# Transposes of the second pair's second norm moved from TensorE to DMA, and a scheduler's price for two-operand work on VectorE set to zero from one point on

## The chip, the cores and the metric

The kernel runs on one core of a Trainium2 chip. A core has TensorE (PE in the profile, its weight loads PEld), VectorE (DVE), ScalarE (ACT), GpSimd (POOL) and SyncE (SP), which here issues all DMAs. The metric is device time of one execution in microseconds (us); of several runs the median counts.

## The reference, cut to what matters

One transformer block with conditioned layer norms, attention over a window of 512 cached keys, and a gated feed forward. Softmax, gelu and silu are the usual ones; c is one row of 512 values.

```python
mod = (silu(c) @ w_mod) -> sa, ca, ga, sb, cb, gb        # six rows of 512
h = layernorm(x) * (1 + ca) + sa                          # x: 2048 x 512
q = h @ wq                                                # 32 heads of 128
s = q @ k[last 512].T / sqrt(128);  p = softmax(s);  o = p @ v[last 512]
x = x + ga * (o @ wo)
h = layernorm(x) * (1 + cb) + sb                          # the second norm
x = x + gb * ((gelu(h @ w_gate) * (h @ w_up)) @ w_down)   # 1376 hidden columns
```

## The kernel before, in words

Every large product runs on TensorE in fp16, with each fp32 operand split into a high part and a low part (value minus high part) and three products for one: high by high, high by low, low by high. Making the parts is work for the other engines. The usual split is a copy to fp16 on ACT and a subtraction of two tensors that lie in SBUF; the function `tt` leaves it to the scheduler whether POOL or DVE does that subtraction.

The 2048 rows are four quarters (`qg` 0 to 3) of 512; quarters 0, 1 are pair 0 and 2, 3 are pair 1. Attention goes over 128 iterations of (head, quarter). An iteration has four times 12 matmuls of 128x512: scores into `psS`, values into `psO`, the output projection into `psW`, the next q into `psQ`. DVE takes the maximum of the scores (`st<-psS`), ACT the exponentials, POOL the low parts of the probabilities (`pp`, 128x1024), SP turns them by DMA transposes (`pT`), DVE and ACT split `oT`, and DVE adds each `psW` to the sum in SBUF (`acc<-psW,st,acc`). There are two banks of `psW`, two pairs of `psS`, one bank of `psO` and of `psQ`: a late evacuation stops TensorE. Beside this the weights of coming heads are scaled, split, and for heads from 2 on combined for a Strassen-Winograd form (`a_sum`, `a_split`, `t_full`, `t_sum`, tiles S, A, tf, T, B).

A weight's scale comes from its largest value over all partitions: the maxima go to DRAM and come back to every partition (`sa`), DVE reduces them (`top`), makes a bounded factor `iv` of four values (line 673) and its reciprocal `av` (line 674). This happens 29 times.

The feed forward works on a pair of quarters at a time. For the second norm of quarters 2 and 3 `ln2_norm` writes the normalized rows in fp32 into tiles of the set T; `ln2_chunk` has TensorE transpose four 128x128 pieces into `psQ`, and ACT or DVE applies the column factors to the result (`hf<-psQ,cols`), then comes the split. It is called through `chunk2` from the table `P1`, in the units of the first pair (lines 1843 to 1847).

Nothing is issued as it is called. The class `Weaver` records every instruction with the tiles it touches, plays the whole program forward by estimated durations, some dozens of times with small random shifts of the urgencies, keeps the play in which most matmul work is done by a number of marks, and issues in that order. Two rules matter here. An instruction may have two engines (`either`); `sooner` holds it back from one engine when the other would end it earlier. And two-operand work on DVE whose operands both lie in SBUF, and all work on POOL, is marked as using one shared port (`lock`): the play lets neither start while the other holds it, and where POOL's instruction follows DVE's closely, it is made to wait for it. To such work on DVE `sooner` adds SHY, 1500 ns, so that DVE gets it only if POOL would end it that much later.

All rows of the profile name line 444, where the recorded instructions are issued, so groups are told apart by their tiles.

Of the kernel before, what the change touches and what calls it, by code (L numbers as in the profile page):

```python
# [10 lines left out]
F32 = mybir.dt.float32  # L11
# [7 lines left out]
P = 128  # L19
N = 512  # L20
# [69 lines left out]
class Weaver:  # L90
# [159 lines left out]
    def play(self, at, users, span, keep, cut):  # L250
# [22 lines left out]
        def sooner(n, e, t):  # L273

            kinds = self.ops[n][4]
            mine = max(t, shared[e] if kinds[e][1] else 0.0) + kinds[e][0] + (e == "DVE" and kinds[e][1]) * self.SHY
            for o, kind in kinds.items():
                s = max(free[o], ready[n], shared[o] if kind[1] else 0.0)
                if o != e and s + kind[0] + (o == "DVE" and kind[1]) * self.SHY < mine:
                    return max(s, t) + 1.0  # L280
            return None

# [169 lines left out]
def adaln_block(ctx: ExitStack, tc: tile.TileContext, x, k_cache, v_cache, wq, wo,  # L452
# [82 lines left out]

    MV, RS, NMR, LNP, LNF = {}, {}, {}, {}, {}

    def ln_stats(key, src, j):
        if j == 0:
            MV[key] = base.tile([P, 4, 2], F32, name="mv", tag="mv", bufs=4)  # L540
            RS[key] = small(base, 4, 4, "rs")
        st = small(base, 6, 2, "bnst")
        nc.vector.bn_stats(st, src)
        nc.vector.bn_aggr(MV[key][:, j, :], st)
        if j == 3:
            ve = small(base, NC, 2, "ve")
            nc.gpsimd.tensor_tensor(ve, MV[key][:, :, 1], eps_t[:, :NC], op=OP.add)
            nc.gpsimd.tensor_tensor(RS[key], ve, eps_t[:, NC:], op=OP.pow)
            nm = NMR[key] = small(base, 4, 4, "nmr")
            nc.gpsimd.tensor_tensor(nm, MV[key][:, :, 0], RS[key], op=OP.mult)  # L550
            nc.gpsimd.tensor_scalar(nm, nm, -1.0, 1.0, op0=OP.mult, op1=OP.mult)
# [115 lines left out]
    def spread_max(t, top):  # L667
        w = right.tile([P, N], F32, name="sa", tag="sa", bufs=1)
        nc.sync.dma_start(w, t.rearrange("p a -> (p a)").partition_broadcast(P))
        r = small(base, 4, 2, "top")  # L670
        nc.vector.tensor_reduce(r, w.rearrange("p (k a) -> p a k", a=4), op=OP.max, axis=AX.X)
        iv, av = small(base, 8, 5, "iv"), small(base, 8, 5, "av")
        nc.vector.tensor_scalar(iv[:, 0:4], r, 1e-30, ROUND / top, op0=OP.max, op1=OP.mult)
        nc.vector.reciprocal(av[:, 0:4], iv[:, 0:4])
        return iv, av

# [592 lines left out]
    def ff_scalars(part):  # L1269
# [12 lines left out]
        if part == 2:  # L1282
            nc.vector.tensor_scalar_mul(t, t, HID)
            nc.vector.reciprocal(ffs[:, 4:5], t)
            nc.vector.reciprocal(ffs[:, 8:9], ab)
            nc.vector.tensor_scalar(cols[:, 8:16], cols[:, 8:16], ffs[:, 8:9], HS, op0=OP.mult, op1=OP.mult)

    s = max(s, 2 * (NIT - 16))
# [49 lines left out]

    N2, FULL, FB, FRAW, AW, WD, WGU, PGU, HID_T, RT, UV, PX = ({} for _ in range(12))
    PLAIN = 2  # L1340
    SLOTS = ("q", "q", "q", "k16", "A1", "A1", "raw2", "raw2")
    SBUFS = {"q": 3, "k16": 1, "A1": 2, "raw2": 2}
    WDTAG = ("kT", "v", "wo", "kT", "kT", "v", "v", "wo", "wo", "oT", "oT")
# [14 lines left out]
        return t[:, 0, c % 2, :], t[:, 1, c % 2, :]  # L1358

    def ln2_stats(qg, j):  # L1360
        ln_stats(("2", qg), acc[4 * qg + j], j)

    def ln2_norm(qg, j):
        if j % 2 == 0:
# [450 lines left out]
        f_low(p, c, "T4")  # L1815

    def chunk2(qg, c):
        ln2_chunk(qg, c)
        ln2_high(qg, c)
        ln2_low(qg, c, nc.vector)  # L1820

# [16 lines left out]
    for c in range(2):  # L1838
# [2 lines left out]


    P1 = {2: [(ln2_stats, 2, j) for j in range(4)] +
          [(ln2_norm, 2, j) for j in range(4)] + [(chunk2, 2, c) for c in range(4)],
          3: [(ln2_stats, 3, j) for j in range(4)] +
          [(ln2_norm, 3, j) for j in range(4)] + [(chunk2, 3, c) for c in range(4)],
          4: [(sums_a, 1, c) for c in range(2)] + [(sums_b, 1, c) for c in range(2)]}
    WDS = list(range(PLAIN, NF))
    left = {(p, h): 2 if h < NF // 2 else 1 for p in range(2) for h in range(NF // 2 + 1)}
# [75 lines left out]
```

## Time and profile before

| | |
|---|---|
| median of 3 runs | 1657.41 us (1656.83 to 1659.0) |
| the profiled execution | 1657.58 us, its span 1655.8 us |
| granted TensorE clock, mean | 0.997 |
| PE busy | 1642.4 us, 99% |
| DVE, ACT, POOL busy | 1289.3, 1216.6, 1305.0 us (78, 73, 79%) |

The span runs from the first to the last instruction. TensorE is busy from start to end, and the other engines are each at about three quarters: what counts is how many instructions TensorE has, and whether one of the others makes it wait. The attention goes from about 40 to 1312 us, the feed forward from there on; in it DMA has little to do.

### The profile page before, as it was taken

What the parts mean: (1) busy time and instruction counts of PE and PEld (TensorE: products, weight loads), DVE (VectorE), ACT (ScalarE), POOL (GpSimd) and SP (SyncE); (2) the same over time, 40 slices, a digit from 0 to 9 for tenths busy, and PEclk for the clock granted to TensorE, in tenths of its full rate; (3) what the DMA queues carried; (4) which work ended last, traced back from release to release, by engine and by line L of the source; (5) the groups of instructions that cost most, each with busy time, mean ns of one, the idle gap of its engine ahead of it and who ended that gap; (6) DMA issues with size and microseconds to landing.
All of it is one profiled execution on the core that took longest, in us unless ns stands there. A gap on an engine that the chain in (4) does not pass through costs nothing.

```text
span 1655.8 us, 24293 instructions
## 1 busy us (share of the span) xinstructions
PE 1642.4 (99%) x7732; PEld 764.5 (46%) x7732; DVE 1289.3 (78%) x2381; ACT 1216.6 (73%) x2418; POOL 1305.0 (79%) x1097
## 2 busy tenths in 40 slices
PE   8999999999999999999999999999999999999999
PEld 4444444444444444444444444444444444444455
DVE  7777787878787788788999887888887956656557
ACT  5987797777787777888778777787878876545451
POOL 5999986868586878787768889999977898784682
PEclk9999999999999999999999999999999999999999
DMA  7676697878787778999999997788877712101111
GB/s 241 128 144 130 135 157 143 152 138 149 144 143 140 153 136 157 186 196 194 196 200 205 189 167 148 147 175 179 168 129 158 144 28 64 42 25 51 42 45 52
DMA packets 686289, 228.61 MB, mean 138 GB/s; under 512 B 596432, under 2 KB 663056, under 8 KB 686160
## 3 DMA queue, kind: packets, MB, share of 16 engines
q1 hardware_dynamic: 686160, 227.05, 69.1%
q8 instruction: 61, 1.00, 0.3%
q14 instruction: 68, 0.56, 0.1%
HBM read 78.98 MB, written 5.38 MB: 51 GB/s over the span
## 4 chain that ended last, share of the span: by engine, by line
PE 91%; ACT 2%; POOL 2%; DVE 2%; DMA 1%; SPq 1%; issue 1%; DVEq 0%; POOLq 0%; ACTq 0%
PE psS L444 31%; PE psW L444 23%; PE psO L444 21%; PE psQ L444 17%; SPq L444 1%; DVE st L444 1%; DVE acc L444 1%; DMA pT<-pp 1%; ACT p L444 0%; POOL pp L444 0%; POOL B L444 0%; DMA wm<-in_w_mod_dram 0%; POOL aw L444 0%; ACT T L444 0%; DMA raw<-in_B_w_up_dram 0%
## 5 line engine op out<-in xcount | busy, mean ns | idle before, releaser
L444 POOL TENSOR_TENSOR pp<-p,pp 128x1024 f16<-128x1024 f32 x256 | 545.9, 2132 | 212.8 <-ACT pp L444 97.3
L444 ACT ACTIVATE p<-psS,st,es 128x512 f32<-128x512 f32 x512 | 393.4, 774 | 187.7 <-DVE st L444 186.8
L444 DVE SCALAR_TENSOR_TENSOR acc<-psW,st,acc 128x512 f32<-128x512 f32 x496 | 367.2, 742 | 79.8 <-PE psW L444 77.7
L444 PE MATMUL psW<-wo,oT 128*128 128x512 f16 x1536 | 416.3, 379 | 0.0
L444 PE MATMUL psS<-kT,q 128*128 128x512 f16 x1536 | 379.1, 379 | 2.0 <-ACT q L444 2.0
L444 PE MATMUL psO<-pT,v 128*128 128x512 f16 x1536 | 377.1, 379 | 0.3 <-DMA pT<-pp 0.2
L444 DVE TENSOR_REDUCE st<-psS 128x2 f32<-128x1024 f32 x256 | 312.5, 1221 | 60.0 <-PE psS L444 59.6
L444 ACT ACTIVATE pp<-p 128x1024 f16<-128x1024 f32 x256 | 271.0, 1059 | 3.7
L444 PEld LDWEIGHTS <-q 128*128 128x128 f16 x1536 | 149.9, 98 | 182.1 <-ACT q L444 2.6
L444 PEld LDWEIGHTS <-v 128*128 128x128 f16 x1536 | 150.0, 98 | 181.3 <-DMA pT<-pp 1.2
L444 PEld LDWEIGHTS <-oT 128*128 128x128 f16 x1536 | 150.2, 98 | 180.1 <-DVE oT L444 0.5
L444 PEld LDWEIGHTS <-aw 128*128 128x128 f16 (+1 forms) x840 | 84.2, 100 | 95.1 <-issue 2.0
L444 ACT ACTIVATE oT<-psO 128x512 f16<-128x512 f32 x128 | 76.1, 594 | 66.2 <-PE psO L444 66.1
L444 PE MATMUL psQ<-T,S 128*128 128x512 f16 x504 | 123.3, 379 | 0.0
L444 PE MATMUL psQ<-B,A 128*128 128x512 f16 x480 | 119.6, 381 | 0.1
L444 PE MATMUL psS<-T,aw 128*128 128x512 f16 (+1 forms) x480 | 116.9, 379 | 0.0
L444 DVE SCALAR_TENSOR_TENSOR oT<-psO,oT 128x512 f16<-128x512 f32 x128 | 88.0, 688 | 30.9 <-ACT oT L444 30.6
L444 PEld LDWEIGHTS <-A 128*128 128x128 f16 x696 | 68.3, 98 | 83.3 <-issue 2.3
L444 PEld LDWEIGHTS <-S 128*128 128x128 f16 x672 | 65.8, 98 | 79.3
L444 ACT ACTIVATION_READ_ACCUMULATOR p<-psS,st,es 128x1 f32 x512 | 101.0, 197 | 0.0
L444 POOL TENSOR_TENSOR q<-h,q 128x512 f16<-128x512 f32 x84 | 97.5, 1161 | 2.0 <-ACT q L444 1.8
L444 DVE TENSOR_REDUCE mx<-raw 128x1 f32<-128x512 f32 x128 | 84.2, 674 | 15.6 <-DMA raw<-in_A_wq_dram 9.1
(211 smaller groups left out, 2295.6 us busy)
## 6 DMA issues: line engine op xcount, KB each, us to landing
raw<-in_A_k_cache_dram SPq DMA_DIRECT2D x32, 256.0 KB, 3.9
raw<-in_A_wq_dram SPq DMA_DIRECT2D x32, 256.0 KB, 3.7
raw<-in_A_v_cache_dram SPq DMA_DIRECT2D x32, 256.0 KB, 3.3
raw<-in_A_wo_dram SPq DMA_DIRECT2D x32, 256.0 KB, 3.2
pT<-pp SPq DMA_TRANSPOSE x512, 3.3
sa<-most SPq DMA_DIRECT2D x29, 256.0 KB, 3.8
raw<-in_B_w_gate_dram SPq DMA_DIRECT2D x24, 256.0 KB, 3.1
raw<-in_B_w_up_dram SPq DMA_DIRECT2D x24, 256.0 KB, 3.4
```

Source lines behind the costliest of these rows:

```text
L444: made[n] = real(*a, **k)
```

## The change

There are three parts.

First, `chunk2` and the table `P1` use new functions for quarters 2 and 3. `turned_norm` normalizes into a tile of the ring p32 (already scaled by HS), copies the high part on ACT and subtracts the low part (POOL or DVE); `turned` has SP transpose both parts by DMA, 16 transposes in all, straight into the tiles that will later hold the feed forward's operand; `turned_chunk` applies the column factors to low and high part (one instruction on ACT or DVE, then a SCALAR_TENSOR_TENSOR on DVE), after which the split is made again as before.

Second, SHY counts only for instructions recorded before `nc.calm`, and `nc.calm` is set to the number of instructions recorded so far. Third, `iv` is made on POOL, while `top` and `av` stay on DVE.

```diff
-            mine = max(t, shared[e] if kinds[e][1] else 0.0) + kinds[e][0] + (e == "DVE" and kinds[e][1]) * self.SHY
+            mine = max(t, shared[e] if kinds[e][1] else 0.0) + kinds[e][0] + (e == "DVE" and kinds[e][1]) * (self.SHY if n < self.calm else 0.0)
...
-                if o != e and s + kind[0] + (o == "DVE" and kind[1]) * self.SHY < mine:
+                if o != e and s + kind[0] + (o == "DVE" and kind[1]) * (self.SHY if n < self.calm else 0.0) < mine:
...
+            if big:
+                nc.gpsimd.tensor_scalar(RS[key], RS[key], HS, 1.0, op0=OP.mult, op1=OP.mult)
...
-        nc.vector.tensor_scalar(iv[:, 0:4], r, 1e-30, ROUND / top, op0=OP.max, op1=OP.mult)
+        nc.gpsimd.tensor_scalar(iv[:, 0:4], r, 1e-30, ROUND / top, op0=OP.max, op1=OP.mult)
         nc.vector.reciprocal(av[:, 0:4], iv[:, 0:4])
...
     PLAIN = 2
+    nc.calm = len(nc.ops)
...
+    def turned_norm(qg, j):
+        if j % 2 == 0:
+            t = b_tile(0, N2TAG[qg][j // 2], (P, 2, 2, 2, N // 2))
+            N2[qg, j], N2[qg, j + 1] = t[:, 0], t[:, 1]
+            RT["norm"] = right.tile([P, 2, N], F32, name="hf", tag="p32", bufs=2)
+        n, t = RT["norm"][:, j % 2, :], N2[qg, j]
+        nc.either((S_, V), lambda o: ln_norm(("2", qg), n, acc[4 * qg + j], j, o))
+        n = n.rearrange("p (a n) -> p a n", a=2)
+        nc.scalar.activation(t[:, :, 0, :], n, AF.Copy)
+        tt(t[:, :, 1, :], n, t[:, :, 0, :], OP.subtract)
+
+    def turned(qg, j):
+        for half in range(2):
+            nm = (("B11", "B21"), ("T4", "B22"))[qg % 2][half]
+            d = ff_b(qg // 2, nm).rearrange("p a c n -> p (a c) n")
+            nc.sync.dma_start_transpose(d[:, :, j * P:(j + 1) * P], N2[qg, j][:, half].rearrange("p a n -> p (a n)"))
+
+    def turned_chunk(qg, c):
...
+        hi, lo = f_view(qg, c)
+        affine(full, lo, a, b)
+        nc.vector.scalar_tensor_tensor(full, hi, a, full, op0=OP.mult, op1=OP.add)
...
     def chunk2(qg, c):
-        ln2_chunk(qg, c)
+        turned_chunk(qg, c)
...
-          [(ln2_norm, 2, j) for j in range(4)] + [(chunk2, 2, c) for c in range(4)],
+          [(g, 2, j) for j in range(4) for g in (turned_norm, turned)] + [(chunk2, 2, c) for c in range(4)],
```

The line `nc.calm = ...` stands where the functions of the feed forward begin. The attention's iterations are recorded further down, by the loop over `slot(i)`; so what is recorded before `nc.calm` is the loads and the work ahead of the first iteration, and the attention lies behind it.

The scheduler makes of this a new order for the whole program. Three places are shown; in names a tile's buffer numbers are mostly left out. On PE, at the end of the attention, the old program has the first of the 32 transposes of quarters 2 and 3 (T_0_3045 and T_0_3046 are quarter 2's normalized rows):

```order
12207 L444 MATMUL psW<-wo,oT 128x512
12208 L444 MATMUL psQ<-ident,T_0_3045 128x128 x2
12209 L444 MATMUL psQ<-ident,T_0_3046 128x128
12210 L444 LDWEIGHTS oT
12211 L444 MATMUL psW<-wo,oT 128x512
```

In the new program no matmul of PE reads these; on SP's queue stand the first 8 of the 16 DMA transposes (T_0_3045 and T_0_3049 are the split rows of quarter 2, B_0_3047 and B_0_3048 the operand), between loads of later weights:

```order
503 L444 DMA_TRANSPOSE B_0_3047<-T_0_3045 128x4x128
504 L444 DMA_TRANSPOSE B_0_3048<-T_0_3045 128x4x128
505 L444 DMA raw<-in_B_w_gate_dram 128x4x128
506 L444 DMA raw<-in_B_w_up_dram 128x4x128
507 L444 DMA raw<-in_B_w_down_dram 128x512
508 L444 DMA raw<-in_B_w_gate_dram 128x4x128
509 L444 DMA raw<-in_B_w_up_dram 128x4x128
510 L444 DMA_TRANSPOSE B_0_3047<-T_0_3045 128x4x128
511 L444 DMA_TRANSPOSE B_0_3048<-T_0_3045 128x4x128
```

The work has changed its engine, and a load behind a transpose on SP now also waits for the split that the transpose reads. The second place is DVE between the 17th and the 18th maximum of the scores, early in the attention; before:

```order
159 L444 TENSOR_REDUCE st<-psS 128x2
160 L444 SCALAR_TENSOR_TENSOR q<-psQ,q 128x512
161 L444 TENSOR_SCALAR st<-st,es 128x1 x2
162 L444 TENSOR_SCALAR acc<-psW,st 128x512
163 L444 SCALAR_TENSOR_TENSOR acc<-psW,st,acc 128x512
164 L444 TENSOR_REDUCE st<-psS 128x2
```

And between the same two maxima now:

```order
185 L444 TENSOR_REDUCE st<-psS 128x2
186 L444 TENSOR_TENSOR tf<-tf 128x512
187 L444 TENSOR_SCALAR st<-st,es 128x1 x2
188 L444 SCALAR_TENSOR_TENSOR acc<-psW,st,acc 128x512
189 L444 TENSOR_TENSOR T_0_90<-tf,T_0_90 128x512
190 L444 TENSOR_TENSOR T_0_88<-tf,T_0_88 128x512
191 L444 SCALAR_TENSOR_TENSOR acc<-psW,st,acc 128x512
192 L444 TENSOR_TENSOR tf<-B_1_93 128x512
193 L444 TENSOR_REDUCE st<-psS 128x2
```

Four sums and splits of the Winograd tiles, which were POOL's, stand on DVE between the evacuations. Counted over the order, DVE has 4 such two-operand instructions (both operands in SBUF, 256 columns or more) in the attention before and 208 now (158 of 512 columns, 50 of 256), 49 of them ahead of the 33rd maximum; in the feed forward it has 87 before and 175 now. POOL goes from 1102 instructions to 862. The third place is POOL around the third of the 29 factors `iv`, between two `pp` of the softmax:

```order
122 L444 TENSOR_TENSOR q<-h_508,q 128x512
123 L444 TENSOR_TENSOR pp<-p_553,pp 128x2x512
124 L444 TENSOR_SCALAR iv<-top 128x4
125 L444 TENSOR_TENSOR pp<-p_567,pp 128x2x512
126 L444 TENSOR_SCALAR raw<-raw,av 128x512 x3
```

And DVE around its reciprocal:

```order
336 L444 TENSOR_REDUCE top<-sa 128x4
337 L444 TENSOR_REDUCE st<-psS 128x2
338 L444 RECIPROCAL av<-iv 128x4
339 L444 TENSOR_SCALAR st<-st,es 128x1 x2
340 L444 SCALAR_TENSOR_TENSOR oT<-psO,oT 128x512
```

`top`, `iv` and `av` followed each other on DVE; now DVE's `av` waits for POOL. Between `top` and `av` stand 0 to 14 other instructions, in 9 of the 29 cases one or none.

## Rows read from the trace of the kernel before

**Rows 1.** The page's busy times: us, share of the span, instructions.
```profile
PE 1642.4 (99%) x7732; PEld 764.5 (46%) x7732; DVE 1289.3 (78%) x2381; ACT 1216.6 (73%) x2418; POOL 1305.0 (79%) x1097
```
**Rows 2.** Stretches: length, busy PE, PEld, DVE, ACT, POOL, clock, DMA share, GB/s.
```profile
0.00:40.00 40.00, 33.54 (x156) 20.08 (x156) 29.06 (x76) 20.76 (x35) 20.25 (x40) 0.91 0.80 250
40.00:200.00 160.00, 158.88 (x752) 73.91 (x753) 120.15 (x234) 134.61 (x267) 155.21 (x119) 1.00 0.70 131
40.00:1312.00 1272.00, 1270.61 (x5900) 577.36 (x5901) 1043.29 (x1993) 1007.24 (x2033) 1041.88 (x785) 1.00 0.83 159
...
1360.00:1600.00 240.00, 239.03 (x1129) 111.64 (x1127) 142.34 (x194) 133.31 (x256) 179.03 (x205) 1.00 0.16 46
```
**Rows 3.** Waits of PE: for what, us in total, times, longest.
```profile
PE psS L444 <- POOL B L444: 0.6, 1, 0.6
PE psS L444 <- ACT r L444: 0.5, 1, 0.5
...
PE psS L444 <- DVE r L444: 0.4, 1, 0.4
```
**Rows 4.** Groups of PE: the transposes of quarters 0, 2 and 3.
```profile
L444 PE MATMUL psQ<-ident,T 128*128 128x128 f32 x48 | 8.1, 275 | 0.0
```
**Rows 5.** Timeline of PE around the last transposes: start, us.
```profile
1416.36 0.60 PE L444 MATMUL psQ<-ident,T 128*128 128x128 f32 x4
1416.80 0.59 PE L444 MATMUL psW<-wd,hid 128*128 128x512 f16 x2
```
**Rows 6.** DVE by tile r and hid: ns shortest/median/longest.
```profile
L444 DVE TENSOR_TENSOR r<-psS,h x60: 676/691/693, 1358.0 to 1635.0; 128x512 f32<-128x512 f32 x54, 96x512 f32<-96x512 f32 x6
L444 DVE TENSOR_TENSOR hid<-r,hid x36: 675/692/1534, 1340.6 to 1643.3; 128x512 f16<-128x512 f32 x32, 96x512 f16<-96x512 f32 x4
L444 DVE SCALAR_TENSOR_TENSOR r<-r,ffs x32: 737/751/1746, 1374.5 to 1641.5; 128x512 f32<-128x512 f32 x28, 96x512 f32<-96x512 f32 x4
```
**Rows 7.** Timeline of DVE and POOL in the feed forward.
```profile
1453.27 1.15 POOL L444 TENSOR_TENSOR T<-hf,T 128x512 f16<-128x512 f32 x1
1453.95 1.02 DVE L444 SCALAR_TENSOR_TENSOR r<-r,ffs 128x512 f32<-128x512 f32 x1
...
1455.11 1.27 POOL L444 TENSOR_TENSOR ft<-ft,hf 128x512 f32<-128x512 f32 x1 [0.69 <-DVE r L444]
...
1455.67 1.27 DVE L444 TENSOR_TENSOR hid<-r,hid 128x512 f16<-128x512 f32 x1
```
**Rows 8.** Timeline of DVE, POOL and PE ahead of PE's wait of 0.60 us.
```profile
1340.63 1.42 DVE L444 TENSOR_TENSOR hid<-r,hid 128x512 f16<-128x512 f32 x1
...
1341.46 1.61 POOL L444 TENSOR_TENSOR T<-hf,T 128x512 f16<-128x512 f32 x1
...
1344.14 1.16 POOL L444 TENSOR_TENSOR B<-hf,B 128x512 f16<-128x512 f32 x1
...
1345.35 0.59 PE L444 MATMUL psS<-B,B 128*128 128x512 f16 x2 [0.60 <-POOL B L444]
```
**Rows 9.** Groups of POOL: busy us, mean ns, idle before.
```profile
L444 POOL TENSOR_TENSOR pp<-p,pp 128x1024 f16<-128x1024 f32 x256 | 545.9, 2132 | 212.8 <-ACT pp L444 97.3 <-issue 91.9 <-DVE acc L444 4.5
L444 POOL TENSOR_TENSOR q<-h,q 128x512 f16<-128x512 f32 x84 | 97.5, 1161 | 2.0 <-ACT q L444 1.8 <-DVE st L444 0.2
```
**Rows 10.** Groups of DVE: addition from psW, score maximum, two-operand work, and iv.
```profile
L444 DVE SCALAR_TENSOR_TENSOR acc<-psW,st,acc 128x512 f32<-128x512 f32 x496 | 367.2, 742 | 79.8 <-PE psW L444 77.7
L444 DVE TENSOR_REDUCE st<-psS 128x2 f32<-128x1024 f32 x256 | 312.5, 1221 | 60.0 <-PE psS L444 59.6
...
L444 DVE TENSOR_TENSOR hid<-r,hid 128x512 f16<-128x512 f32 x32 | 28.3, 897 | 4.3 <-ACT hid L444 4.1
...
L444 DVE TENSOR_SCALAR iv<-top 128x4 f32<-128x4 f32 x29 | 6.1, 211 | 0.0
```
**Rows 11.** DMA issues: count, median us to landing.
```profile
pT<-pp SPq DMA_TRANSPOSE x512, 3.3
```
**Rows 12.** Groups of ACT: a split's high part.
```profile
L444 ACT ACTIVATE T<-hf 128x512 f16<-128x512 f32 x16 | 10.0, 624 | 3.1 <-POOL hf L444 2.9
```

More of the change, by code (lines that the diff above doesn't have):

```diff
@@ L536, in adaln_block, with ln_stats @@
     MV, RS, NMR, LNP, LNF = {}, {}, {}, {}, {}
-    def ln_stats(key, src, j):
+    def ln_stats(key, src, j, big=False):
         if j == 0:
@@ L1285, in ff_scalars @@
             nc.vector.reciprocal(ffs[:, 8:9], ab)
+            nc.vector.tensor_scalar_mul(ffs[:, 9:13], cols[:, 8:12], ffs[:, 8:9])
             nc.vector.tensor_scalar(cols[:, 8:16], cols[:, 8:16], ffs[:, 8:9], HS, op0=OP.mult, op1=OP.mult)
@@ L1360, in ln2_stats @@
     def ln2_stats(qg, j):
-        ln_stats(("2", qg), acc[4 * qg + j], j)
+        ln_stats(("2", qg), acc[4 * qg + j], j, qg in TURNED)
+    TURNED = (2, 3)
+    def turned_norm(qg, j):
[14 more added lines that the diff above has]
+    def turned_chunk(qg, c):
+        if c % 2 == 0:
+            RT["full"] = right.tile([P, 2, N], F32, name="hf", tag="p32", bufs=2)
+        full = FULL[qg, c] = RT["full"][:, c % 2, :]
+        a, b = ffs[:, 9 + c:10 + c], colB[2][:, c:c + 1]
+        hi, lo = f_view(qg, c)
+        affine(full, lo, a, b)
+        nc.vector.scalar_tensor_tensor(full, hi, a, full, op0=OP.mult, op1=OP.add)
     def ln2_norm(qg, j):
@@ L1843, in adaln_block @@
     P1 = {2: [(ln2_stats, 2, j) for j in range(4)] +
-          [(ln2_norm, 2, j) for j in range(4)] + [(chunk2, 2, c) for c in range(4)],
+          [(g, 2, j) for j in range(4) for g in (turned_norm, turned)] + [(chunk2, 2, c) for c in range(4)],
           3: [(ln2_stats, 3, j) for j in range(4)] +
-          [(ln2_norm, 3, j) for j in range(4)] + [(chunk2, 3, c) for c in range(4)],
+          [(g, 3, j) for j in range(4) for g in (turned_norm, turned)] + [(chunk2, 3, c) for c in range(4)],
           4: [(sums_a, 1, c) for c in range(2)] + [(sums_b, 1, c) for c in range(2)]}
```

## The prediction

> **What bounds the kernel now.** I read the page first [rows 1]. TensorE is busy for 1642.4 us, 99% of the span. The stretches come next [rows 2]: in the attention, 40 to 1312 us, TensorE lacks 1.4 of 1272 us; from 1360 to 1600 us it lacks 1.0. In that attention DVE is busy 82% and POOL 82%, in the feed forward DVE 59% and POOL 75%. So the time is TensorE's own instructions, and an edit counts only if it takes instructions from TensorE or makes it wait. Waits of TensorE in the feed forward are three, of 0.6, 0.5 and 0.4 us, 1.5 us in all [rows 3].
>
> **Transposes: minus 3.5 us.** Each of quarters 2 and 3 has four chunks of four transposes: 32 leave TensorE, the only matmuls that go. Their group has a mean of 275 ns [rows 4], but that is the time from start to the end of the drain: four start at 1416.36 and the next matmul at 1416.80 [rows 5], which is 0.11 us of TensorE for one. 32 x 0.11 = 3.5 us. Their group has no idle time before it [rows 4], so nothing else of theirs lay on the path. The Trainium skill (TensorE: Matmul & The Clock Gate, Part 4: PE-mode transpose) gives about 275 ns for a transpose inside a kernel, mostly access latency; as an estimate from that page 32 would return 8.8 us. The rows agree with 275 ns as a duration and not as a cost, since the engine goes on after 0.11 us; the sum goes by the spacing.
>
> **What replaces them: 0 on the path.** Eight copies on ACT at 0.62 us as any high part [rows 12], eight more subtractions and eight SCALAR_TENSOR_TENSOR on DVE or POOL, 16 transposes on SP. On ACT that is 5 us in 240 us of which it works 133 [rows 2]. A DMA transpose lands after 3.3 us [rows 11]; here several instructions follow each other (norm, split, transpose, two for the factors, split), perhaps 8 us more from norm to operand than with TensorE. The old chunks were turned by 1416.36 [rows 5], while TensorE first reads the second pair's operand some 24 us of its own work later by its order. That cover hides it; without it the price would be those 8 us once. On SP the loads of weights for later units stand behind transposes that wait for a split. The DMA engines are 16% busy there [rows 2], so a load that starts some us late still lands in 3; I take 0.
>
> **The two-operand work: plus 1.5 us, the uncertain term.** By the order 204 more such instructions stand on DVE in the attention and 88 more in the feed forward, 292 in all. As `nc.calm` is set before the attention is recorded, the larger part moves there, where DVE had the least room. One takes 0.69 us when nothing disturbs it (the median of `hid`), against 1.16 on POOL [rows 6, 9]. In the attention 154 of 512 columns are 106 us; 50 of half the size, taken as half of it plus some overhead, about 20; the 29 `iv` of 0.21 us leave [rows 10]. DVE goes from 1043 to some 1163 of 1272 us, 91%, and POOL to some 830. On average there is room. DVE idles 77.7 us in the attention before additions to `acc`, waiting for the matmul [rows 10]: evacuations now start as soon as they can, and part of this margin goes.
>
> What comes on top is the port. At 1453.95 a DVE instruction of two SBUF operands took 1.02 us instead of its median of 0.75, beside one of POOL that ended at 1454.42; at 1455.67 another took 1.27 instead of 0.69, beside one of POOL that ended at 1456.38 [rows 6, 7]. Both ended 0.55 us after POOL's. `hid` has a median of 692 and a longest of 1534 ns, while `r<-psS,h`, with one operand in PSUM, never passes 693 [rows 6]. `hid` at 897 in the mean [rows 10] is 0.2 us a piece over its median. POOL suffers in turn: its subtraction took 1.61 instead of 1.16 us behind DVE's, the next chain ended at 1345.30, and TensorE lost 0.60 us [rows 8]. The Trainium skill (SBUF — State Buffer, Who interferes with whom) says that a DVE instruction with two SBUF inputs and a GpSimd instruction that reads SBUF take the shared pair as an exclusive lock for the whole instruction. The rows agree, and by that rule one DVE instruction could stand for a whole `pp`.
>
> How much of that reaches TensorE no row shows for the attention. From below: nothing, if the order leaves enough margin at each place; it may even fall by the 1.5 us of waits in the feed forward that POOL's lighter load can remove, so minus 1.5. From above: all three waits put to the 87 such instructions that stand in the feed forward now, 1.5 / 87 = 17 ns each, times 292, plus 5.0 us. Only one of the three was made by the port, and of it the 0.45 us by which POOL's subtraction was stretched: 0.45 / 87 x 292 = 1.5 us. I take that, since it is the row nearest to the mechanism.
>
> **`iv` on POOL: 0.** It saves 6 us of DVE [rows 10]. It adds a wait: DVE's reciprocal now waits for POOL, with the score maxima and evacuations queued behind it, and ACT's exponentials behind these. Where POOL is inside a `pp`, that can be 2.13 us [rows 9]. Where two or more instructions stand between on DVE (20 of 29) they cover about 1.5 us. The other 9 are a rival below.
>
> **Sum.** 1657.58 of the profiled execution - 3.5 + 1.5 = 1655.6; the median lies 0.17 below that execution, so 1655.4 us. The new random shifts also give another order ahead of the first iteration, where TensorE lacks 6.5 of 40 us [rows 2]; that can be a microsecond either way, and is in the range only.
>
> **Rivals.** *All is hidden and the waits close.* POOL loses about 240 instructions, and in the feed forward it was the busiest of the three; the 1.5 us of waits can go with the 3.5: 1657.4 - 5.0 = 1652.4. For it: the old order left TensorE only 1.4 us short in the whole attention. Against it: the margins that did this were DVE's idle time, and this shrinks.
>
> *DVE becomes the bound early in the attention (slower).* From 40 to 200 us POOL was busy 155 of 160 us and DVE 120 [rows 2]. 49 of the moved instructions stand ahead of the 33rd maximum, in this stretch: 49 x 0.67 = 33 us, so DVE has 153 of 160 us before any port wait. Between the 17th and 18th maximum the new order has 5.9 us on DVE (1.22 for the maximum, 4 x 0.69, 2 x 0.74 for the additions, and two small ones at 0.2 like `iv` [rows 6, 10]), where TensorE needs 5.2 for 24 matmuls (5900 took 1270.6 [rows 2]). The point from which it decides is 0.14 us of port wait for each of the 49. At the 0.2 of `hid` it is 163 of 160; `hid` met POOL instructions of 1.2 us, and these meet `pp` of 2.13, about twice as long [rows 9], so perhaps 0.4: 173 of 160. Less 4 us because instructions of DVE overlap a little at their ends, TensorE would be 9 us late: 1657.4 - 3.5 + 9 = 1663. Against it: a rule in the scheduler passes over such work while the port is taken, and the 87 instructions of the feed forward cost little.
>
> *The reciprocal waits.* In 9 places nothing or one instruction covers it; at half a `pp` each that is 9.6 us of DVE, and if half of it reaches TensorE: 1655.4 + 4.8 = 1660.2. For it: the order puts `iv` between two `pp`; against it, the schedule placed each `iv` with POOL's work in view.
>
> *The price of zero only reaches the feed forward*, as its name says. The order speaks against it; then 88 x 5 ns = 0.5 us: 1654.4. It is part of the forecast's range.
>
> **How the numbers follow.** 0.2% is 3.3 us, about what a measurement of this kernel tells from no change: faster is below 1654.1, slower above 1660.7. The forecast has 0.45, its own range is 1653 to 1657.5, with 0.08 of it below 1654.1; all hidden 0.27; DVE as the bound 0.23; the reciprocal 0.05. Faster 0.27 + 0.08 = 0.35, within 0.37 + 0.05 = 0.42, slower 0.23. The range goes from 1651 (all hidden, and a microsecond from the start) to 1663.
>
> **What would show it.** In the new profile: 32 fewer 128x128 f32 matmuls on PE; waits of TensorE for DVE in the attention of 1 to 2 us in sum, and some DVE subtractions of `q`, `v`, `wo`, `k` over 1 us beside `pp`; DVE at about 91% of the attention. If PE's busy time is not about 3.5 us shorter, the first term is wrong. If PE waits for DVE above 4 us, most of it ahead of 200 us, DVE is the bound. If TensorE waits for an operand of the second pair after 1430 us, the cover of the transposes was too thin. A `RECIPROCAL` with idle time before it put to POOL would show the last wait.

## The result, and the profile after

The changed kernel takes 1660.56 us (median of 22 runs, 1656.01 to 1666.51), the kernel before 1657.47 us (22 runs, 1656.05 to 1659.83) on the same chip: a ratio of 1.0018, 95% interval 1.0012 to 1.0023. It is slower by 3.1 us, where 2.0 us faster was forecast, and its runs spread over 10.5 us, those of before over 3.8. The profiled execution took 1660.08 us, its span 1658.3 us at a mean clock of 0.999. All times and ratios here and below are of fast executions; three that took 1913 to 4511 us, in the runs of e13, e16 and of the kernel before beside e17, are left out.

The page's busy times first, in the form of [rows 1]:

```profile
PE 1638.7 (99%) x7700; PEld 760.4 (46%) x7700; DVE 1446.0 (87%) x2642; ACT 1224.0 (74%) x2424; POOL 1035.9 (62%) x857
```

TensorE has 32 matmuls fewer and is busy 3.7 us less, and yet the span is 2.5 us longer. DVE has gained 157 us, POOL has lost 269. The stretches of [rows 2], and one of 40 us in the feed forward:

```profile
40.00:200.00 160.00, 158.53 (x748) 73.14 (x746) 150.19 (x287) 133.11 (x268) 113.01 (x80) 1.00 0.73 138
40.00:1312.00 1272.00, 1267.48 (x5878) 574.99 (x5876) 1143.03 (x2152) 1003.29 (x2017) 848.03 (x612) 1.00 0.83 158
1360.00:1600.00 240.00, 237.50 (x1110) 109.19 (x1108) 185.60 (x267) 141.25 (x268) 118.30 (x152) 1.00 0.20 52
1420.00:1460.00 40.00, 37.51 (x172) 16.44 (x170) 39.18 (x63) 29.57 (x52) 8.67 (x9) 1.00 0.24 58
```

The same 40 us in the kernel before:

```profile
1420.00:1460.00 40.00, 39.95 (x185) 17.98 (x184) 26.38 (x33) 17.39 (x31) 33.31 (x30) 1.00 0.15 40
```

In the attention TensorE lacks 4.5 us where it lacked 1.4. In 1420 to 1460 us DVE has gone from 26.4 to 39.2 of 40 us, POOL from 33.3 to 8.7, and TensorE lacks 2.5 us.

Busy time hides small gaps, so I measured them from the starts: from each matmul to the next, less the spacing that such a matmul has when nothing is late (0.216 us for 128x512 in fp16, 0.11 us for a transpose or half the columns). The sum of what is left is called lost time here. Before, it is 16.2 us, after 22.3; the work itself goes from 1634.1 to 1630.6 us. That is -3.5 + 6.1 = +2.6 us, where the spans differ by 2.5. Of the 6.1 us, 5.3 lie between 50 and 1300 us (0.2 before, 5.5 now) and 2.0 between 1400 and 1500 us (1.4, now 3.4); the start is 0.9 us better, the rest 0.3 better.

What TensorE waits for, in the whole span (rows of the ramp at the start left out):

```profile
PE psW L444 <- DVE acc L444: 1.9, 5, 0.7
...
PE psO L444 <- DVE wd L444: 1.5, 1, 1.5
PE psO L444 <- DMA pT<-pp: 1.4, 2, 1.1
...
PE psQ L444 <- DVE q L444: 0.7, 2, 0.5
PE psO L444 <- DVE acc L444: 0.6, 1, 0.6
```

These names are nearly all DVE's, with values of 0.5 to 1.5 us, where [rows 3] had POOL, ACT and DVE with at most 0.6. Groups of the new kernel that answer to [rows 4, 10], with DVE's reciprocal:

```profile
L444 DVE SCALAR_TENSOR_TENSOR acc<-psW,st,acc 128x512 f32<-128x512 f32 x496 | 367.5, 743 | 34.2 <-PE psW L444 31.7
...
L444 POOL TENSOR_SCALAR iv<-top 128x4 f32<-128x4 f32 x29 | 6.6, 228 | 37.0 <-DVE top L444 30.0 <-DVE ga L444 4.6 <-DVE st L444 1.4
...
L444 DVE RECIPROCAL av<-iv 128x4 f32<-128x4 f32 x29 | 5.1, 175 | 1.0 <-POOL iv L444 0.9
...
L444 PE MATMUL psQ<-ident,T 128*128 128x128 f32 x16 | 3.1, 276 | 0.0
```

DVE's idle time ahead of the additions to `acc`, the margin in the attention, has gone from 79.8 to 34.2 us. The reciprocal waits 0.9 us for POOL in all. The largest loss of the feed forward, in order of time:

```profile
1450.45 0.70 POOL L444 TENSOR_TENSOR aw<-S4f,aw 128x256 f16<-128x256 f32 x1 [2.84 <-DVE r L444]
...
1450.55 1.15 DVE L444 TENSOR_TENSOR T<-hf,T 128x512 f16<-128x512 f32 x1
...
1451.62 0.68 DVE L444 TENSOR_TENSOR ft<-hf,ft 128x512 f32<-128x512 f32 x1
1452.23 0.74 DVE L444 SCALAR_TENSOR_TENSOR wd<-raw,ffs,wd 128x512 f16<-128x512 f32 x1
...
1453.02 0.38 PE L444 MATMUL psO<-wd,hid 128*128 128x512 f16 x1 [1.46 <-DVE wd L444]
...
1455.52 1.16 POOL L444 TENSOR_TENSOR T<-ft,T 128x512 f16<-128x512 f32 x1 [4.37 <-DVE hf L444]
```

TensorE stands 1.46 us for `wd`, which only DVE may make. It stands in DVE's queue behind two-operand work of the second pair that POOL may do as well, while POOL does nothing from 1451.15 on, for 4.37 us. A port wait of the kind that the prediction priced has a part in it: the first of DVE's instructions here took 1.15 us where its kind takes 0.68, beside POOL's of 0.70 us, and ended 0.55 us after it. That is up to 0.47 of the 1.46 us.

### The profile page after: what moved, and what is told of

Read it like the earlier page. It is cut to its first block, busy times and chain, and to the rows that moved or that the text cites. A ratio compares the mean times of both kernels' runs of the same rounds, so it can differ in the third digit from the quotient of the medians.

```text
span 1658.3 us, 24348 instructions
## 1 busy us (share of the span) xinstructions
PE 1638.7 (99%) x7700; PEld 760.4 (46%) x7700; DVE 1446.0 (87%) x2642; ACT 1224.0 (74%) x2424; POOL 1035.9 (62%) x857
## 5 line engine op out<-in xcount | busy, mean ns | idle before, releaser
L444 PE MATMUL psW<-wo,oT 128*128 128x512 f16 x1536 | 466.9, 379 | 1.9 <-DVE acc L444 1.9
L444 PE MATMUL psS<-kT,q 128*128 128x512 f16 x1536 | 404.9, 379 | 1.3 <-ACT q L444 1.3
L444 PE MATMUL psO<-pT,v 128*128 128x512 f16 x1536 | 404.4, 379 | 1.4 <-DMA pT<-pp 1.4
L444 DVE SCALAR_TENSOR_TENSOR acc<-psW,st,acc 128x512 f32<-128x512 f32 x496 | 367.5, 743 | 34.2 <-PE psW L444 31.7
L444 PE MATMUL psQ<-T,S 128*128 128x512 f16 x504 | 137.0, 379 | 0.7 <-DVE q L444 0.7
L444 PE MATMUL psQ<-B,A 128*128 128x512 f16 x480 | 128.8, 379 | 0.0
L444 PE MATMUL psS<-T,aw 128*128 128x512 f16 (+1 forms) x480 | 121.1, 379 | 0.0
L444 PE MATMUL psS<-B,aw 128*128 128x512 f16 (+1 forms) x360 | 90.1, 379 | 0.0
```

What stands on the lines that cost most here:

```text
L444: made[n] = real(*a, **k)
```

## The experiments

The three parts are called turned (transposes by DMA), price (SHY zero from `nc.calm` on) and iv. The column of medians is the median less that of the kernel before, taken on the same chip beside it. The last columns are lost time by stretch (us) in the one profiled execution of each kernel, which need not lie at its median: e7's took 1665.37 us, the longest of its seven, 3.1 us above their median.

| kernel | median | ratio, interval | 50-1300 | 1300-1400 | 1400-1500 |
|---|---|---|---|---|---|
| before | | | 0.2 | 0.9 | 1.4 |
| after | +3.1 | 1.0018 (1.0012-1.0023) | 5.5 | 0.6 | 3.4 |
| e1 turned | +14.2 | 1.0083 (1.0069-1.0097) | 0.6 | 2.0 | 16.3 |
| e2 price | +11.6 | 1.0069 (1.0055-1.0083) | 4.7 | 9.0 | 0.0 |
| e3 iv | +2.1 | 1.0016 (1.0007-1.0025) | 2.8 | 0.5 | 1.3 |
| e4 all, price behind attention | +4.7 | 1.0028 (1.0019-1.0038) | 5.6 | 0.1 | 4.6 |
| e5 before, draw 8 | -0.2 | 0.9996 (0.9987-1.0006) | 2.3 | 0.8 | 1.8 |
| e6 after, draw 8 | +1.8 | 1.0012 (1.0003-1.0022) | 6.3 | 0.3 | 2.8 |
| e7 turned, price | +4.6 | 1.0027 (1.0016-1.0038) | 6.4 | 0.4 | 6.0 |
| e8 turned, draw 8 | +11.4 | 1.0067 (1.0052-1.0082) | 0.8 | 2.2 | 14.2 |
| e9 turned, price behind attention | +0.5 | 1.0000 (0.9990-1.0010) | 2.3 | 0.1 | 4.9 |
| e10 after, price 500 | +5.1 | 1.0033 (1.0020-1.0046) | 4.1 | 0.9 | 6.6 |
| e11 as e9, price 500 | +2.9 | 1.0020 (1.0011-1.0030) | 2.6 | 0.1 | 7.4 |
| e12 after, broadcast +3 us | -1.1 | 0.9992 (0.9982-1.0001) | 3.3 | 0.7 | 2.0 |
| e13 before, broadcast +3 us | +4.9 | 1.0031 (1.0018-1.0043) | 5.9 | 0.8 | 2.2 |
| e14 as e9, broadcast +3 us | +1.2 | 1.0005 (0.9996-1.0013) | 2.0 | 0.0 | 5.9 |
| e15 as e12, draw 8 | -0.7 | 0.9996 (0.9987-1.0005) | 2.5 | 0.1 | 2.9 |
| e16 as e12, without iv | +4.8 | 1.0028 (1.0017-1.0040) | 6.7 | 0.6 | 5.4 |
| e17 before, broadcast +1.5 us | +2.2 | 1.0014 (1.0006-1.0023) | 0.7 | 1.8 | 1.9 |
| e18 after, broadcast +1.5 us | +5.6 | 1.0037 (1.0023-1.0051) | 7.7 | 0.2 | 4.5 |

**Each part alone.** e1 is the changed kernel with two lines taken back:

```diff
-    nc.calm = len(nc.ops)
+    nc.calm = 1 << 60
-        nc.gpsimd.tensor_scalar(iv[:, 0:4], r, 1e-30, ROUND / top, op0=OP.max, op1=OP.mult)
+        nc.vector.tensor_scalar(iv[:, 0:4], r, 1e-30, ROUND / top, op0=OP.max, op1=OP.mult)
```

> The transposes moved to DMA, with the price of 1500 ns kept everywhere and iv on DVE. Theory (the price is what costs): TensorE's instructions are 3.5 us shorter, its gaps stay at the 16 us of before, of which some 0.9 us lie behind the first 50 us in the attention and 1.5 us between 1400 and 1500 us; 1653 to 1655 us. Rival 1 (the longer way through the DMA makes the gaps of 2 to 3 us at 1451 us): these gaps are there too, 1656 to 1657. Rival 2 (each new order is a draw of the search, worth some us either way): anything from 1651 to 1658, with gaps at other places than in the changed kernel.

Neither the theory nor a rival had this: 14.2 us more. The lost time lies in the feed forward, 16.3 us of it. The stretch, and the chain at its largest gap:

```profile
1420.00:1460.00 40.00, 29.59 (x126) 12.39 (x125) 25.74 (x31) 24.95 (x44) 32.35 (x28) 0.96 0.28 69
```

```profile
1426.77 1.19 SPq L444 DMA_TRANSPOSE B<-T  x1
...
1428.01 3.88 SPq L444 DMA_TRANSPOSE T<-T  x3
...
1434.56 2.57 SPq L444 DMA_TRANSPOSE B<-T  x2
...
1435.85 1.52 ACT L444 ACTIVATE hf<-T,cols,ffs 128x512 f32<-128x512 f16 x2 [5.67 <-DMA T<-T]
1436.70 0.75 DVE L444 SCALAR_TENSOR_TENSOR hf<-T,ffs,hf 128x512 f32<-128x512 f16 x1 [5.27 <-ACT hf L444]
1437.17 0.58 SPq L444 DMA_DIRECT2D raw<-in_B_w_gate_dram  x1
...
1438.16 1.68 PE L444 MATMUL psW<-wd,hid 128*128 128x512 f16 x5 [3.15 <-DVE acc L444]
```

The transposes go one after the other, and each waits for its split, which waits for POOL (32 of 40 us busy). ACT stands 5.67 us in line for the turned tile, DVE 5.27 us for ACT, and the addition that would free a bank for TensorE stands behind DVE's instruction. The loads of weights come on SP only at 1437.17. What I had as a latency hidden by 24 us of other work is a chain that holds four queues (SP, ACT, DVE and with them TensorE).

e2 has the price alone:

```diff
+    TURNED = ()
-        turned_chunk(qg, c)
+        ln2_chunk(qg, c)
-          [(g, 2, j) for j in range(4) for g in (turned_norm, turned)] + [(chunk2, 2, c) for c in range(4)],
+          [(ln2_norm, 2, j) for j in range(4)] + [(chunk2, 2, c) for c in range(4)],
```

(the same for quarter 3, and `iv` on DVE).

> The price of zero alone: transposes on TensorE, iv on DVE. Theory: the attention gets some 5 us of gaps of TensorE instead of 1, DVE busy about 90% of it, and the feed forward some 2 us more; 1662 to 1665 us. Rival 1 (the DMA way makes the gaps at 1451 us): the feed forward keeps its 1.5 us; 1660 to 1662. Rival 2 (a draw): 1654 to 1660.

It comes out above the theory's 1665 us: 4.7 us of lost time in the attention, as the theory had, and 9.0 at the start of the feed forward, which it did not have. There 3.9 of the 9.0 us stand ahead of TensorE's own transposes, which it now comes to before ACT has made their rows or emptied their bank; the rest are waits for operands of the first pair and the like:

```profile
1362.00 0.33 PE L444 MATMUL psQ<-ident,T 128*128 128x128 f32 x1 [0.69 <-ACT T L444]
...
1363.28 0.33 PE L444 MATMUL psQ<-ident,T 128*128 128x128 f32 x1 [0.95 <-ACT T L444]
...
1367.30 0.66 PE L444 MATMUL psQ<-ident,T 128*128 128x128 f32 x4 [0.65 <-ACT hf L444]
```

e3 has `iv` on POOL alone (`nc.calm = 1 << 60`, `TURNED = ()`).

> iv on POOL alone. Theory: it costs nothing, 1656.5 to 1658.5 us, and no wait of TensorE behind an av. The rival of the prediction (the reciprocal waits for POOL, and maxima and additions behind it): DVE shows idle time before av put to POOL, and the time is 2 to 5 us more, 1659 to 1662. A draw of the search: 1655 to 1660.

At +2.1 us the time lies at the near end of the rival's 2 to 5, and a draw is not excluded. DVE's reciprocals wait 3.2 us for POOL here, the longest 1.2 us, but none of TensorE's gaps over 0.3 us in the attention follows such a wait within 5 us.

The three parts alone add to 14.2 + 11.6 + 2.1 = 27.9 us; together they cost 3.1. Each part makes most of the other's loss in the feed forward go: in e7, which has both, 0.4 us is left of the 9.0 and 6.0 of the 16.3. My reading, which no run takes apart: with turned, TensorE's queue holds nothing that waits for the norm; with the price, the splits behind the DMA transposes need not wait for a busy POOL.

e4 sets `nc.calm` behind the loop over `slot(i)`, all else as changed:

```diff
-    nc.calm = len(nc.ops)
+    nc.calm = 1 << 60
...
     hooks(2 * (NIT + 4) + 0.5)
+    nc.calm = len(nc.ops)
     assert not bg, bg
     plain_act((0, 1))
```

> All of the change, but the price becomes zero only for what is recorded behind the attention's iterations (the mark is set after their loop). Theory (most of the loss is in the attention, some in the feed forward): the 5 us of gaps in the attention go, the 2 us more between 1400 and 1500 us stay; 1655 to 1656.5 us. If the feed forward's loss came of what the attention leaves behind: 1653 to 1654.5. A draw of the search: 1651 to 1659.

This is slower than any of its forecasts: the attention keeps 5.6 us of lost time though DVE is as idle there as before. Its load, and the largest gap of the attention:

```profile
40.00:1312.00 1272.00, 1268.06 (x5880) 575.12 (x5879) 1039.68 (x1957) 1014.17 (x2029) 1039.58 (x804) 1.00 0.82 158
```

```profile
911.96 0.52 DVE L444 TENSOR_REDUCE mff<-raw 128x1 f32<-128x352 f32 x1 [2.31 <-DMA raw<-in_B_w_up_dram]
...
913.12 0.68 DVE L444 SCALAR_TENSOR_TENSOR oT<-psO,oT 128x512 f16<-128x512 f32 x1
...
913.86 0.38 PE L444 MATMUL psO<-pT,v 128*128 128x512 f16 x1 [1.23 <-DVE oT L444]
```

DVE stands 2.31 us at a maximum of a weight that has not landed; the split of `oT`, which TensorE needs, is behind it. The load of DVE is not the only way to lose time.

**The draw.** e5, e6 and e8 begin the planner's random shifts at 8 for 7, in before, after and e1.

```diff
-        draw = random.Random(7)
+        draw = random.Random(8)
```

> The kernel before, whole, only the start of the planner's random draw changed (8 for 7): the same instructions, in another plan. Theory of the change (the added time comes from what the parts do to the engines): before's gaps of TensorE are small because its work is well spread, so another draw gives them again, 1656 to 1660 us. Rival (each plan is a lucky or unlucky draw, and before was a lucky one): 1659 us or more, no better than the changed kernel.

> The changed kernel, whole, with the draw started at 8 for 7. Theory: the gaps in the attention (about 5 us beyond those before) and in the feed forward (2 to 4 us) come back in other places, 1659 to 1663 us, 0.1 to 0.4% above before. Rival (draw): anywhere from 1654 us (the 3.5 us of the transposes gained and nothing lost) to 1663 us.

> Transposes by DMA alone, draw started at 8. With the draw at 7 this part cost 14 us, 16 us of gaps in the stretch 1400 to 1500 us. Theory (a chain of norm, split, SP's transposes and factors, with the weights' loads behind the transposes in SP's queue, too long while GpSimd has its share of the two-operand work): the gaps stay within a few us, 1666 to 1676 us. Rival (one bad draw): most of them go, 1656 to 1661 us.

All three come out as their theory had it (the rival of e6, anywhere from 1654 to 1663 us, is not excluded), and another draw gives the same picture: before 1657.45, after 1659.45, turned alone 1669.05 us. In e6 TensorE's waits between 50 and 1300 us are two kinds:

```profile
PE psQ L444 <- DVE q L444: 4.1, 4, 1.7
PE psW L444 <- DVE acc L444: 1.3, 2, 1.0
```

The whole list of the kernel before in that stretch is this row:

```profile
PE psO L444 <- DMA pT<-pp: 0.2, 1, 0.2
```

And one of the four in e6, in DVE's and TensorE's order:

```profile
353.75 1.07 DVE L444 TENSOR_REDUCE top<-sa 128x4 f32<-128x512 f32 x1 [3.62 <-DMA sa<-most]
355.18 0.18 DVE L444 RECIPROCAL av<-iv 128x4 f32<-128x4 f32 x1 [0.35 <-POOL iv L444]
355.27 0.72 DVE L444 SCALAR_TENSOR_TENSOR acc<-psW,st,acc 128x512 f32<-128x512 f32 x1
355.91 0.68 DVE L444 SCALAR_TENSOR_TENSOR q<-psQ,q 128x512 f16<-128x512 f32 x1
...
356.64 0.59 PE L444 MATMUL psQ<-T,S 128*128 128x512 f16 x2 [1.66 <-DVE q L444]
```

DVE stands 3.62 us at the reduce, waiting for the broadcast of the maxima to land; an addition and the split of q, which frees the only bank of `psQ`, stand behind it, and TensorE waits 1.66 us. All four gaps over 0.45 us in this kernel's attention follow such a stand of 1.94 to 3.62 us, 2.4 to 3.5 us after DVE goes on. Four of e7's five do too (1.48 to 2.82 us), and two of the changed kernel's six (1.94 us at this reduce; 1.26 us at another maximum, which waits for POOL). Of its other four, two wait for `pT`, and ahead of two DVE simply has no idle time: from 190.33 us on its instructions follow each other, until TensorE stands here:

```profile
196.97 0.38 PE L444 MATMUL psW<-wo,oT 128*128 128x512 f16 x1 [0.66 <-DVE acc L444]
```

The DVE instructions in e6's rows have their usual lengths. Port waits do happen in the changed kernel's attention: from 50 to 1300 us 15 of DVE's 196 instructions with two wide SBUF operands took over 0.9 us. The longest, which TensorE did not wait for:

```profile
947.82 1.73 DVE L444 TENSOR_TENSOR v<-raw,v 128x512 f16<-128x512 f32 x1
```

None of the 15 lies in the 7 us ahead of any of the six gaps.

**Which part.** e7 is the changed kernel with `iv` on DVE (second pair of lines of e1's diff).

> The change without its third part: transposes by DMA and price zero, iv on VectorE as before. Theory that iv on GpSimd costs the attention its gaps (with it alone there were 2.5 us more than before): those go, 1656 to 1659 us. Rival (price zero from the attention on moves two-operand work to VectorE, whose queue then stands behind a late operand): the attention keeps 4 to 5 us of gaps, 1660 to 1663 us.

e9 is e4 with `iv` on DVE as well.

> Transposes by DMA, price zero only for what is written behind the attention's loop, iv on VectorE: the changed kernel's feed forward behind the attention of the kernel before. Theory (the attention's 5 us of added gaps come from the price and from iv; the transposes' 3.5 us stay gained): gaps of about 1 us in 50 to 1300 us, of 3 to 5 us in 1400 to 1500 us, 1655 to 1658 us. Rival (the gaps in the attention come with any new plan): 4 us or more of gaps there again, 1659 to 1662 us.

For e7 the rival is right. e9's time is the theory's, with 2.3 us of lost time in the attention where it had 1. e7 and e9 differ only in where the price begins: +4.6 and +0.5 us, 6.4 and 2.3 us of lost time in the attention. `iv` has no sign of its own: on POOL it costs with the price behind the attention (e9 to e4, +4.2 us) and gains with the price in it (e7 to after, -1.5). Put together, with turned, the attention loses 2.3 us with neither (e9), 5.6 with `iv` alone (e4), 6.4 with the price alone (e7) and 5.5 with both (after): either of the two suffices, and both cost no more than one.

**A price between.** e10 and e11 write 500 for zero in both lines of the price, in the changed kernel and in e9.

```diff
-(self.SHY if n < self.calm else 0.0)
+(self.SHY if n < self.calm else 500.0)
```

> The whole change with a price of 500 where it has zero. Theory (at zero GpSimd is left 4 of 20 us busy while VectorE has 20 of 20 in 1430 to 1450 us, and TensorE waits for VectorE there): GpSimd takes a share again, over 8 of 20 us, VectorE falls under 18, the gaps of 1400 to 1500 us go under 2 us, 1656 to 1660 us. Rival (the pair of engines holds one port, so what GpSimd takes VectorE loses, as with transposes by DMA alone): gaps of 6 us and more there, 1662 us or more.

> Transposes by DMA, price 500 only behind the attention's loop, iv on VectorE. Theory: the attention of before (gaps of about 1 us) and a feed forward whose two-operand work is shared out (gaps under 2 us in 1400 to 1500 us): 1653 to 1656 us, faster than the kernel before. Rival (a chain through norm, split and transposes too long for any price above zero): 6 us of gaps or more in 1400 to 1500 us, 1658 to 1665 us.

The rival is right in both. In e10:

```profile
1420.00:1460.00 40.00, 36.03 (x157) 15.47 (x156) 38.32 (x53) 28.06 (x48) 17.57 (x16) 0.96 0.26 57
```

POOL works twice as long as in the changed kernel, and DVE ends 53 instructions in 38.3 us, 0.72 each, where it ended 63 in 39.2, 0.62 each. Much of what POOL takes is given back in longer instructions of DVE. The Trainium skill (SBUF — State Buffer, Who interferes with whom) says that whichever of the two takes the shared pair first blocks the other for its whole instruction; these rows agree, by 0.72 us against 0.62. Part of e10's lost time is the clock, 0.96 in this row (last section).

**The broadcast counted later.** e12 tells the planner that a transfer that reads back from DRAM what the kernel wrote there, `sa` above all, lands 3 us later than it had assumed, so that the reduce goes behind other work. The end of the line, before and in e12:

```diff
-end + 1500.0 * (m in self.landing))
+end + (4500.0 if m >= self.calm else 1500.0) * (m in self.landing))
```

> The whole change, but the planner counts the broadcast of the weights' maxima (the transfer into sa) as landing 3 us later, so that VectorE's queue has its reduce (top from sa) behind other work. Theory (TensorE's added gaps in the attention come from VectorE standing at that reduce: 11.6 us idle at 11 of 29 in the changed kernel, 7.2 at 8 before): the idle time there falls under 4 us, and the gaps of 50 to 1300 us from 6 to under 3 us; 1656 to 1658 us. Rival (those stalls are hidden, VectorE is late because it has 100 us more work): the gaps stay at 5 us or more, 1659 to 1662 us.

The kernel comes to 1656.07 us, 4.5 us under the changed one (4.2 when each is taken against the kernel before on its own chip). DVE's waits for the broadcast between 50 and 1300 us, in the changed kernel and in e12 (us in total, times, longest):

```profile
DVE top L444 <- DMA sa<-most: 11.6, 11, 2.2
```

```profile
DVE top L444 <- DMA sa<-most: 6.7, 6, 1.8
```

The direction is the theory's, its size was not: I had said under 4 us here and under 3 of lost time, which is 3.3. Part of the 4.5 us lies in the feed forward, 1.4 us, where no broadcast is.

e13 is the same edit in the kernel before, e14 in e9 (counted from the same place, with the price still behind the attention); e15 is e12 with draw 8, e16 is e12 with `iv` on DVE.

> The kernel before, only with the broadcast of the weights' maxima counted as landing 3 us later in the attention: a control. Theory (with GpSimd taking its share VectorE has over 200 us free in 1272 of the attention, and its stalls at the reduce behind the broadcast are mostly hidden): 1656 to 1658 us, within 0.1% of before. Rival (counting the broadcast later is worth 1 to 4 us to any kernel, and says nothing of the price): 1653 to 1655.5 us.

> Transposes by DMA, price zero only behind the attention's loop, iv on VectorE, and the broadcast counted 3 us later. Without the last this was 0.5 us above before. Theory: gaps in 50 to 1300 us fall from 2.3 to 1 us, those of 1400 to 1500 us stay at 3 to 5, 1655 to 1657 us. Rival (the attention gives nothing more, its gaps are late transposes): 1657 to 1659 us.

> The whole change with the broadcast counted 3 us later, the planner's draw started at 8. Theory: with the draw at 7 the later count gave 4.5 us against the changed kernel; it gives 2 us or more against the changed kernel with the draw at 8 as well, 1655 to 1657.5 us, with VectorE idle under 7 us ahead of the reduce (13.7 there) and gaps under 4.5 us in 50 to 1300 us (6.3 there). Rival (a lucky draw): 1658.5 to 1661 us.

> Transposes by DMA, price zero from the attention on, broadcast counted 3 us later, iv left on VectorE. Theory that iv on GpSimd is worth about the 1.5 us that lay between the change with and without it: 1657 to 1659 us. Rival (with iv on GpSimd two hand-overs more are on the chain behind the reduce, so that without it the kernel is faster): 1654 to 1656 us.

e15 repeats e12, as its theory had. e14 changes little, as its rival had. e13 is 4.9 us slower than before and e16 4.8, which neither of their theories nor rivals had. e16 loses 3.4 us more than e12 in the attention and 3.4 more in 1400 to 1500 us, where no `iv` is made. So I ran the middle of both rows, 3000 for 4500:

> The kernel before with the broadcast counted as landing 1.5 us later (3 us later made it 5 us slower, which neither theory had). Theory (that count makes the chain of a head's weights longer in the plan, which a kernel whose GpSimd is the fuller engine pays): something between, 1658 to 1661 us, with 2 to 5 us of gaps in 50 to 1300 us. Rival (the 5 us were one bad plan): 1656 to 1657.5 us.

> The whole change with the broadcast counted 1.5 us later, half of the step that gave 4.5 us. Theory (VectorE stands less ahead of its reduce the later the plan counts the broadcast): between the changed kernel and that one, 1656.5 to 1659.5 us, 3 to 5.5 us of gaps in 50 to 1300 us. Rival (plans scatter by some us whatever the count): outside of that.

Before goes 0, +2.2, +4.9 us with the count, the theory's time, though with 0.7 us of lost time in the attention where it had 2 to 5; the changed kernel goes +3.1, +5.6, -1.1. For the latter the rival holds: plans of the same instructions scatter by some us, and that e12 is fast is not shown to be the count's doing. Two draws are not two independent plans: the gaps of e12 and e15 stand at the same places (near 184, 597 and 919 us).

**Over the plans.** Eight kernels have the price at zero in the attention (after, e2, e6, e7, e12, e15, e16, e18): lost time there 2.5 to 7.7 us, mean 5.4. Nine have neither that nor `iv` on POOL (before, e1, e5, e8, e9, e11, e13, e14, e17): 0.2 to 5.9, mean 1.9. In 1400 to 1500 us ten have turned with the price at zero (after, e4, e6, e7, e9, e12, e14, e15, e16, e18): 2.0 to 6.0, mean 4.2; five have the transposes on TensorE and the old price (before, e3, e5, e13, e17): 1.3 to 2.2, mean 1.7. The sum over plans is -3.5 + 3.5 + 2.5 = +2.5 us, near the 3.1 measured, and one plan lies up to some 3 us off its mean. The groups differ in other parts too, so the two terms are means and not prices of one edit.

Three pairs differ, as far as the attention goes, only in the price there, with `iv` on DVE: before and e2, e9 and e7, e14 and e16. The lost time in the attention rises by 4.5, 4.1 and 4.7 us. With `iv` on POOL (e4 and after) it does not, -0.1, and `iv` without the price adds 2.6 (before to e3) and 3.3 (e9 to e4).

The traces of these groups also test the way by DVE's stands. Counted are DVE's waits of 1.2 us or more for a DMA, from 50 to 1300 us, and gaps of TensorE over 0.45 us (by lost time) within 5 us behind them. In the eight kernels with the price 24 of 46 stands have such a gap behind them, in the nine with neither price nor `iv` on POOL 5 of 29. In the eight 25 of 42 gaps, and 27 of 40 us in them, come so. For the rest no one way is shown; e13, where DVE is no busier than before, loses 5.9 us in the attention, and none of its four gaps stands behind such a wait.

## Why the prediction was wrong

*Transposes, minus 3.5 us*: right. 32 matmuls went, and the work at nominal spacing fell by 3.5 us; the 275 ns of a transpose are again a duration (276).

*The two-operand work, plus 1.5 us, the uncertain term*: this step failed. The time lost in the attention rose by 5.3 us, above the term's upper bound of 5.0, and the mechanism was another. The prediction put TensorE's loss to single port waits and sized it from the one such wait of the feed forward; such waits are there in the attention (15 instructions of DVE over 0.9 us, up to 1.73), and none stands ahead of the larger gaps of TensorE there. DVE's share was forecast well (1163 of 1272 us; 1143). But DVE works in order, and some of its instructions wait for a transfer or for another engine. Such stands were there before the change and no shorter (the changed kernel has 11.6 us of them at this reduce, longest 2.2). In the kernel before, from 50 to 1300 us:

```profile
DVE mx L444 <- DMA raw<-in_A_wq_dram: 9.1, 5, 2.2
DVE top L444 <- DMA sa<-most: 7.2, 8, 2.2
```

With DVE idle 18% of the attention they reached TensorE nowhere in this kernel, and in 5 of 29 cases over the nine plans; at 10% in 24 of 46. The price was to be read from these waits, which the prediction left out, and not from `hid`. That this is the way in e6 and e7 is read from their traces. For the changed kernel it covers two gaps of six, two more stand behind a DVE without idle time, and for its two waits for `pT` no cause is shown. That the price alone makes such a loss, 4 to 5 us, is shown by three pairs; but the changed kernel would have it without the price as well, from `iv` on POOL (e4, 5.6 us).

*What replaces them, 0 on the path*: wrong too. The cover of 24 us was counted for one latency; e1 shows 16.3 us of lost time with the old price. Under the new price 2.0 us remain in the changed kernel, some 2.5 over the plans, where DVE is full from 1420 to 1460 us, and not, as I named it, in waits of TensorE for an operand of the second pair. With the price but without the DMA transposes (e2) DVE has 32.9 of these 40 us and no time is lost from 1400 to 1500 us: the price alone does not fill DVE there.

*`iv`, 0*: wrong without the price in the attention, where `iv` on POOL costs 2.1 us (e3) and 4.2 (e9 to e4); right or better with it (-1.5). The way that I feared is not it: the reciprocals wait 0.9 us in all in the changed kernel, and in e3, where they wait 3.2, no gap of TensorE follows. Why it costs is open; the new plan that comes with it is the rival.

*DVE becomes the bound early* (slower, 1663): the right sign in the wrong place. In 40 to 200 us DVE has 150.19 of 160 us, near the 153 forecast, but of the attention's 5.5 us of lost time only 1.7 lie ahead of 200 us; that rival's own test asked for most of it. DVE is full in 1420 to 1460 us, where the old profile had it at 66%: the prediction divided 88 instructions over a whole feed forward, and 30 more instructions than before stand in these 40 us (63, then 33).

*All is hidden* did not happen: with POOL relieved the feed forward's lost time grew, since DVE was then full where POOL had been.

*The new order* was in the range only for the start, at a microsecond. It scatters the whole kernel by some 3 us, as much as the change. The changed kernel's own executions scatter as widely (1656.01 to 1666.51 us), and each has one trace. The faster versions, e12 and e15, cannot be told from before.

## What to carry to other kernels

Before work is moved to an engine with 18% idle, list what that engine waits for in its own queue: each such stand must be covered by slack behind it. Here, in the kernels with the price, more than half of the gaps of TensorE stood behind such stands. Test parts of a change together as well as alone: here 14, 12 and 2 us alone became 3 together. Where a search makes the order, run a change in several plans of both kernels, and take the mean, before a difference of a few us is called the change's.

## What the runs showed of the hardware

A stand of TensorE can cost more than its length. In e11 TensorE waited 3.47 us for `hid`; the granted clock of the stretches around it (the figure behind POOL's, ahead of the DMA share) was:

```profile
1448.00:1452.00 4.00, 3.71 (x18) 1.56 (x17) 4.00 (x8) 1.35 (x3) 2.58 (x3) 1.00 0.00 0
1452.00:1456.00 4.00, 0.53 (x3) 0.11 (x2) 4.00 (x8) 2.08 (x4) 0.00 (x0) 1.00 0.00 0
1456.00:1458.00 2.00, 2.00 (x8) 0.84 (x7) 2.00 (x4) 1.02 (x2) 0.00 (x0) 0.73 0.00 0
1458.00:1460.00 2.00, 2.00 (x7) 0.63 (x5) 2.00 (x5) 0.57 (x1) 0.00 (x0) 0.50 0.00 0
1460.00:1462.00 2.00, 2.00 (x10) 0.91 (x9) 1.92 (x4) 1.27 (x3) 1.16 (x1) 0.92 0.00 0
```

It fell to 0.50, the lower level of 1.2 GHz, about a microsecond after the wait had ended, and matmuls start 0.43 us apart until 1459.98. The 21 spacings from 1455.87 to 1462.10 take 6.23 us; at 0.216 they would take 4.54, so the wait cost another 1.7 us. The waits of 1.46 us in the changed kernel and of 2.23 us in e6 left it at 1.00. The same fall stands in e1, e7, e8, e10, e14 and e16, each time behind waits of TensorE; in e10 in this row:

```profile
1456.00:1458.00 2.00, 2.00 (x6) 0.73 (x5) 2.00 (x4) 0.93 (x2) 0.46 (x1) 0.50 0.00 0
```

So the lost time of these kernels in 1400 to 1500 us (5.4 to 16.3 us in the table) is not waits alone.

The 16 DMA transposes of 128x512 fp16 go on SP one after the other at 1.2 to 1.3 us each, and land after 2.5 us (12 of them, by the changed kernel's list of DMA issues), less than the 3.3 us of [rows 11].
